# Attention with a window, then a token-mixing MLP: 1,143 steps in another written-out order

## The chip, the cores and the metric

The kernel runs on one core of a Trainium2 chip. A core has engines that run side by side, each with its own list of instructions that it works off in order: TensorE (PE in the profile; its weight loads are PEld), VectorE (DVE), ScalarE (ACT), GpSimd (POOL) and SyncE (SP), which only issues DMAs. ScalarE and GpSimd issue DMAs too. An engine waits for another by semaphores. The metric is the device time of one execution in microseconds (us), over several executions.

## What is computed

```python
# attention: B=4, H=8, S=768, D=64; window 128, 4 sink positions
scores = q @ k.T / sqrt(D)
keep = (key < 4) | ((0 <= query - key) & (query - key < 128))
a = softmax(where(keep, scores, -1e9))
x = a @ v                                   # heads side by side: (4, 768, 512)
...
a1 = alpha1 * x + beta1
tok = einsum('ts,bsd->btd', w_tok, a1)      # w_tok 768 x 768
u = x + lam * tok
a2 = alpha2 * u + beta2
ch = relu(a2 @ w_ch1) @ w_ch2               # 512 -> 2048 -> 512
out = u + lam * ch
```

Inputs and output are float32; the matmuls work on float16.

## The kernel before

The body of the kernel is a plan of 1,143 small steps, called tasks and numbered in the order in which they are described. A task is one load, one cast, a group of matmuls into one PSUM buffer, one exponential, one copy and the like. `Plan.add` describes it: what function it runs, on which engines it may run, which tasks it needs, which buffers it uses. `Plan.emit` (lines 57 to 82) walks through the tuple `ORDER` (line 216) and issues the tasks one by one. The string `ENGINES` (line 287) has one digit for each task: 0 ScalarE, 1 VectorE, 2 TensorE, 3 GpSimd, 4 SyncE. So an engine's list is `ORDER` with the other engines' tasks left out; where two neighbours in `ORDER` are on two engines, their exchange changes no list. Waits follow from the data.

The string `HOMES` (line 302) gives each buffer a slot. A buffer in a slot waits until the last user of the one before it in that slot is done. PSUM has four slots of kind `d` (`d0` to `d3`: transposes, attention output, MLP results) and two of kind `S` (scores). `n16` is a kind of SBUF buffer (four slots) in which casts of q, k and w_tok are put. `IDLES` (line 312) lays dummy matmuls on TensorE ahead of five tasks: 67 and 25 in the first 9 us, two ahead of task 109, in slot `d3`, and four and one near 28 us.

How the work runs, batch by batch:

- Queries and keys are loaded (`load_qk`, 384 KB each), cast to float16 (`trans`, line 157 on VectorE and GpSimd, 155 on ScalarE) and transposed: by TensorE (lines 508 and 511) and a copy from PSUM for batches 0 and 1, by a DMA for batches 2 and 3.
- Scores (`scores`, line 621; for the start of batch 0 in pairs, lines 682 and 685) go into an `S` slot, ScalarE takes the exponential (line 643), and the mask is put on by GpSimd (583) or VectorE (658). `pv` (lines 715, 722) multiplies by the values; VectorE divides (748). `fill_vs` (line 572) makes, by a selection matrix, the values of the sink positions.
- The token mixing (`tok`, line 853) takes 6 matmuls for each of 6 row blocks; VectorE adds (860), the result is cast to `u` (155) and transposed to `uT`, by TensorE in batch 0, by a DMA (line 912) after that, and scaled (877, 879).
- The MLP's first half (`mlp1`, line 933) makes 16 pieces of `h` for each half of the rows, four matmuls each, in a `d` slot that a relu on ScalarE (939) or VectorE (941) reads and frees. The second half is `ch` (line 1118) in batch 0; in batches 1 to 3 it is done as seven products of sums of blocks (`prod`, line 1050), in the manner of Strassen.
- The second weight comes in eight loads and is multiplied by lam in 16 pieces, `cast_w2` (line 835), each on VectorE or GpSimd. `w2_sums` (line 965) makes the sums of its blocks (`w2s`) for the products.

The four batches overlap: scores and attention of batch b+1 are laid between the MLP matmuls of batch b.

Tasks named later:

| task | what it is | engine before |
|---|---|---|
| 2 | biases from the masks (line 352) | VectorE |
| 54 | copy of a transposed k, head pair 1, batch 0 | ScalarE |
| 63 | cast of v, row blocks 0 and 1, batch 0 | VectorE |
| 43 | transpose of alpha2 and beta2 | TensorE |
| 53, 55, 59 | transposes of q and k, batch 0 | TensorE |
| 92, 95, 103, 109, 111 | scores, batch 0 | TensorE |
| 153, 157 | adding lb1 to x, batch 0 (two of `beta`) | VectorE |
| 183, 184, 202 | multiplications of w2 by lam, pieces 2, 3 and 15 | VectorE, VectorE, GpSimd |
| 262, 266, 284 | relus of batch 0 | VectorE |
| 240, 270 | relus of batch 0 | ScalarE |
| 269, 299 | `h` of batch 0, four matmuls each | TensorE |
| 352, 353 | two of the `w2s` subtractions, of groups 2 and 3 | VectorE, GpSimd |
| 372, 381 | casts of q and k, batch 1 | GpSimd |
| 395 | selection matmul of `fill_vs`, batch 1 | TensorE |
| 472 | token mixing of batch 1, row block 3, six matmuls | TensorE |
| 660 | scores of batch 2, block 1 | TensorE |
| 621 | load of a k of batch 2 | ScalarE's queue |
| 899 | cast of a k of batch 3 | ScalarE |

The lines that do the issuing:

```python
for i in order:
    t = self.tasks[i]
    e = (ACT, DVE, PE, POOL, SP)[int(engines[i])]
    ...
    for b in t.uses:
        if b.t is None:
            ...
            b.t = pool.tile(b.shape or shape, b.dtype or dtype,
                            tag=f"{b.kind}_{b.home}", bufs=1, name=b.name)
    t.fn(e)
```

Of the kernel before, what the change touches and what calls it, by code (L numbers as in the profile page):

```python
# [77 lines left out]
def kernel(  # L78
# [119 lines left out]
    for r in range(NR):  # L198
# [15 lines left out]
    PAIRS = 3  # L214

    ORDER = (
        6, 7, 0, 26, 1, 10, 5, 9, 11, 45, 18, 8, 2, 19, 48, 3, 22, 46, 15, 4, 49, 12, 50,
        17, 14, 47, 13, 16, 90, 103, 39, 41, 91, 43, 104, 53, 72, 95, 54, 28, 63, 96, 51,
        42, 73, 52, 74, 109, 100, 21, 40, 107, 44, 110, 20, 68, 108, 65, 61, 55, 92, 56, 24,
        97, 93, 101, 98, 69, 111, 94, 102, 59, 30, 62, 99, 113, 23, 57, 114, 112, 25, 116,  # L220
        105, 58, 60, 115, 27, 128, 106, 64, 131, 129, 135, 130, 125, 66, 132, 31, 138, 29,
        78, 122, 179, 117, 178, 136, 139, 126, 118, 119, 197, 140, 123, 127, 137, 120, 32,
        146, 141, 133, 84, 33, 70, 134, 79, 147, 34, 85, 144, 71, 80, 124, 86, 150, 142, 67,
        75, 35, 154, 143, 121, 151, 76, 155, 158, 148, 145, 77, 87, 152, 166, 159, 156, 81,
        167, 162, 88, 160, 163, 82, 89, 168, 149, 213, 164, 83, 153, 209, 217, 157, 214,
        218, 210, 229, 219, 211, 215, 212, 226, 165, 216, 230, 220, 161, 223, 36, 222, 232,
        221, 224, 185, 225, 177, 227, 176, 257, 169, 204, 237, 175, 233, 279, 238, 199, 234,
        258, 273, 280, 231, 259, 228, 274, 171, 277, 182, 260, 186, 241, 278, 246, 172, 200,
        295, 248, 247, 174, 291, 296, 181, 187, 243, 293, 170, 292, 242, 289, 294, 384, 267,
        188, 290, 37, 281, 268, 198, 271, 349, 282, 173, 285, 272, 358, 301, 351, 286, 180,  # L230
        378, 303, 352, 297, 302, 189, 203, 304, 249, 366, 379, 192, 190, 250, 298, 287, 369,
        380, 385, 283, 288, 375, 386, 367, 353, 265, 284, 368, 206, 370, 191, 266, 363, 376,
        381, 371, 253, 377, 299, 254, 372, 364, 300, 382, 201, 365, 373, 615, 275, 374, 383,
        205, 261, 276, 183, 357, 387, 408, 262, 263, 409, 184, 202, 395, 264, 269, 614, 411,
        239, 410, 412, 397, 240, 270, 388, 621, 396, 235, 400, 617, 196, 244, 398, 401, 355,
        255, 616, 245, 236, 390, 256, 193, 360, 389, 251, 399, 207, 311, 252, 391, 359, 335,
        393, 195, 392, 424, 208, 636, 426, 622, 194, 312, 648, 425, 336, 427, 634, 394, 428,
        413, 419, 414, 404, 420, 337, 405, 429, 402, 415, 313, 361, 422, 416, 626, 421, 441,
        305, 403, 442, 638, 640, 423, 406, 314, 619, 430, 315, 437, 443, 431, 316, 435, 641,
        338, 436, 362, 438, 306, 649, 341, 317, 432, 618, 433, 407, 637, 444, 307, 345, 439,  # L240
        644, 339, 318, 445, 620, 635, 434, 628, 450, 308, 451, 639, 440, 452, 446, 453, 417,
        642, 319, 645, 447, 340, 323, 418, 643, 320, 309, 448, 658, 623, 321, 324, 449, 322,
        329, 625, 659, 454, 646, 325, 347, 647, 330, 455, 343, 326, 344, 464, 456, 465, 348,
        466, 460, 650, 457, 467, 327, 458, 331, 629, 461, 459, 462, 653, 632, 651, 463, 656,
        332, 654, 356, 652, 660, 627, 333, 310, 342, 472, 38, 655, 624, 480, 473, 468, 469,
        470, 474, 885, 665, 471, 476, 475, 481, 482, 488, 477, 350, 483, 492, 489, 478, 490,
        657, 630, 493, 479, 514, 491, 516, 328, 515, 882, 518, 663, 880, 517, 879, 498, 666,
        661, 664, 502, 519, 499, 508, 346, 512, 662, 509, 678, 513, 484, 671, 679, 486, 676,
        503, 504, 485, 487, 354, 877, 506, 677, 672, 548, 507, 680, 526, 505, 549, 334, 674,
        546, 527, 631, 522, 681, 907, 547, 528, 523, 903, 534, 633, 529, 675, 682, 878, 890,  # L250
        535, 542, 683, 689, 543, 550, 685, 690, 510, 551, 686, 494, 511, 673, 667, 544, 495,
        891, 668, 496, 545, 901, 669, 888, 883, 693, 497, 897, 687, 684, 530, 688, 694, 700,
        531, 524, 670, 696, 701, 500, 525, 698, 697, 501, 691, 552, 699, 558, 553, 695, 704,
        562, 705, 904, 692, 559, 707, 909, 563, 706, 709, 887, 708, 564, 898, 710, 702, 566,
        565, 910, 715, 567, 703, 713, 716, 532, 714, 889, 520, 533, 717, 538, 537, 521, 921,
        539, 556, 540, 536, 557, 560, 541, 718, 899, 922, 572, 711, 881, 884, 574, 573, 896,
        712, 902, 576, 561, 719, 577, 575, 555, 727, 720, 569, 721, 580, 908, 728, 578, 581,
        729, 722, 723, 905, 579, 554, 730, 739, 568, 724, 592, 740, 725, 582, 570, 911, 726,
        588, 593, 583, 912, 584, 595, 571, 743, 731, 906, 589, 732, 585, 590, 733, 605, 900,
        587, 744, 596, 745, 606, 734, 594, 607, 611, 597, 895, 602, 612, 586, 613, 599, 603,  # L260
        591, 757, 600, 759, 758, 601, 741, 765, 742, 771, 766, 760, 916, 772, 746, 751, 917,
        773, 752, 886, 913, 761, 919, 774, 604, 767, 918, 598, 762, 763, 768, 777, 764, 779,
        920, 914, 780, 923, 915, 755, 778, 926, 608, 756, 924, 930, 735, 609, 927, 925, 931,
        753, 736, 781, 893, 737, 928, 892, 782, 934, 738, 929, 775, 935, 754, 932, 941, 610,
        769, 776, 819, 770, 894, 942, 939, 820, 821, 940, 937, 936, 823, 749, 822, 748, 945,
        824, 938, 747, 827, 933, 948, 950, 750, 943, 952, 951, 825, 953, 787, 828, 944, 807,
        788, 797, 826, 949, 808, 946, 829, 954, 798, 801, 830, 791, 802, 947, 956, 792, 783,
        957, 961, 789, 784, 962, 958, 963, 955, 790, 785, 959, 964, 811, 965, 805, 812, 786,
        795, 806, 960, 967, 796, 799, 793, 968, 970, 966, 813, 794, 969, 971, 972, 814, 815,
        973, 809, 800, 816, 974, 803, 810, 978, 804, 976, 979, 837, 975, 977, 835, 838, 980,  # L270
        841, 836, 818, 839, 843, 842, 840, 981, 845, 832, 982, 846, 817, 986, 983, 844, 831,
        990, 987, 851, 991, 988, 984, 833, 847, 992, 834, 855, 993, 848, 1002, 852, 849,
        985, 998, 1003, 989, 856, 1004, 850, 859, 1005, 1006, 860, 853, 997, 868, 995, 1007,
        996, 999, 865, 1008, 858, 857, 1000, 1009, 862, 869, 866, 874, 1001, 994, 854, 1016,
        863, 875, 1040, 1017, 871, 1041, 1038, 872, 1020, 1039, 1028, 1021, 1011, 1032,
# [2 lines left out]
        1061, 1048, 1014, 1049, 1059, 1066, 1015, 1044, 1067, 1072, 1045, 1056, 1073, 1026,  # L278
        1057, 1078, 1068, 1079, 1064, 1069, 1046, 1027, 1063, 1052, 1047, 1050, 1053, 1082,
        1051, 1062, 1084, 1083, 1065, 1030, 1080, 1085, 1101, 1031, 1081, 1091, 1102, 1107,  # L280
        1092, 1097, 1093, 1105, 864, 867, 1108, 1098, 1103, 1106, 1111, 1104, 1113, 1112,
        1089, 1114, 1115, 1086, 1116, 1090, 861, 1094, 1087, 1109, 1099, 1121, 1100, 1117,
        1095, 1110, 1125, 1118, 1122, 1134, 1124, 1123, 1126, 1128, 1135, 1127, 1088, 1119,
        1136, 1120, 1140, 873, 876, 1129, 1131, 1096, 1141, 1142, 1137, 1130, 1132, 1133,
        1138, 1139,
    )
    ENGINES = (
        "3313134433443333444444444444444433334443111211211212020212021201331121211210210200201210"
        "2020201202011202020202020213213213213213213202002020202020213121312131213121312131444444"
        "4444413114433334413314413334444042210221021021020121321021321202020020211212020202020212"  # L290
        "1212020212120202120212020212121202020202022221022221422221022221422221022221013111111331"
        "1311333333302002002132132002132002102020101212010321213120301212131201012121312010121213"
        "1203212131212131213421342104011121042104213400012120202021202021212120202020212120202121"
# [6 lines left out]
        "202020112020212021202020112020210202142141111212121212121211121112131210210214214214210"  # L300
    )
    HOMES = (
        "145602340010102001213310200221013302203140101100511203013144215120821000003330a501103130"
        "5140011112031102051467032311003221123033120133001001232002203212113003321023113113103113"
        "20311022642130030020210002112300123001450093004101001b3002014531200000131101000502017200"
        "3206010112033310021331123331330302113210001232150012232123130221212022310345033723010320"
        "103100135301020081002011411421050103321a003101204000011011051003031104020013001303110312"
        "0021102210121102223200511310123320031102032021035337572302312010320101420152002210101311"
# [1018 lines left out]
```

## Time and profile before

| | |
|---|---|
| runs before, us | 256.24, 257.22, 257.45 |
| median, us | 257.22 |
| profiled execution, us | 256.29 |
| its span (first to last instruction), us | 254.2 |
| granted TensorE clock | 0.998 |
| DMA traffic | 38.79 MB, mean 153 GB/s |

The profile cuts the span in 40 slices of 6.4 us; each digit is the busy share of a slice in tenths:

```
PE   8899999999999998999999999999999999999992
DVE  6878987778788975688889986677789885029892
ACT  2499944788986015687742445556660234643000
POOL 8527915996866516433872040066562130000010
```

Windows of 10 us of TensorE's busy time: 10.00 from 50 to 60 us, 9.64 from 60 to 70, 9.27 from 90 to 100, 10.00 from 100 to 110.

How it is read: a row of a timeline has the start, the duration, the engine, the line, the operation, what it writes and reads, and a count where several of one form follow each other. In square brackets stand the idle time before it and what ended that. Matmul records overlap, as the engine is pipelined: the step from one start to the next is what a matmul costs the list, not its record. The time of a run is some 2 us more than the span.

### The profile page before, as it was taken

The page shows a single profiled execution, that of the slowest core. Times are in us where ns is not written, and L with a number is a line of the kernel's source. Part 1 is how long each engine was busy: PE and PEld are TensorE (multiplying, and loading weights), DVE is VectorE, ACT ScalarE, POOL GpSimd, SP SyncE. Part 2 cuts the span into 40 slices and gives each one's busy share as a digit, 9 for nine tenths or more (in the row PEclk, how much of TensorE's full clock was granted, in tenths as well). Part 3 has the DMA queues.
Part 4 walks back from the last instruction along what each step waited for, and adds up shares of the span by engine and source line. Part 5 has one row for each costly group of instructions (what it writes and reads, how often), then busy time and mean ns, then how long its engine had stood idle before and what let it go on. Part 6 is the DMA issues. An engine that isn't in the chain of part 4 may idle for free.

```text
span 254.2 us, 5511 instructions
## 1 busy us (share of the span) xinstructions
PE 245.8 (97%) x2167; PEld 160.2 (63%) x2167; DVE 194.0 (76%) x400; ACT 132.5 (52%) x219; POOL 108.4 (43%) x126
## 2 busy tenths in 40 slices
PE   8899999999999998999999999999999999999992
PEld 7654655675555443566687686577577676667882
DVE  6878987778788975688889986677789885029892
ACT  2499944788986015687742445556660234643000
POOL 8527915996866516433872040066562130000010
PEclk9999999999999999999999999999999999999999
DMA  6999999999999997696476764320000141100317
GB/s 196 207 253 322 253 206 326 372 341 250 223 179 235 221 182 170 141 256 153 107 163 138 104 144 138 124 64 0 3 0 3 25 79 23 41 0 3 132 55 270
DMA packets 86129, 38.79 MB, mean 153 GB/s; under 512 B 73540, under 2 KB 80460, under 8 KB 86104
## 3 DMA queue, kind: packets, MB, share of 16 engines
q1 hardware_dynamic: 67120, 28.85, 47.7%
q10 hardware_dynamic: 15240, 6.32, 10.2%
q0 software_dynamic: 3744, 3.28, 8.1%
q8 instruction: 17, 0.28, 0.5%
q14 instruction: 8, 0.07, 0.1%
HBM read 29.91 MB, written 6.29 MB: 142 GB/s over the span
## 4 chain that ended last, share of the span: by engine, by line
PE 87%; ACT 3%; DVE 3%; DMA 3%; POOL 1%; issue 1%; POOLq 0%; ACTq 0%; DVEq 0%
PE h L933 31%; PE P L1050 22%; PE tok L853 12%; PE ch L1118 8%; PE pv L722 4%; PE S L621 4%; DMA n<-in_q_dram 3%; PE S L616 1%; PE tp L511 1%; ACT E L643 1%; ACT wt L818 1%; PE tp L508 1%; PE pv L715 1%; PE wT L813 1%; DVE w2f L835 1%
## 5 line engine op out<-in xcount | busy, mean ns | idle before, releaser
L933 PE MATMUL h<-uT,w1f 128*128 128x384 f16 x512 | 89.8, 326 | 0.4 <-DVE x L860 0.3
L933 PEld LDWEIGHTS <-w1f 128*128 128x128 f16 x512 | 48.2, 98 | 31.8 <-issue 2.2
L939 ACT ACTIVATE hT<-h 128x384 f16<-128x384 f32 x77 | 36.9, 493 | 36.2 <-PE h L933 36.0
L941 DVE TENSOR_SCALAR hT<-h 128x384 f16<-128x384 f32 x51 | 27.5, 553 | 22.6 <-PE h L933 22.2
L1050 PEld LDWEIGHTS <-hT 128*128 128x128 f16 x408 | 39.5, 98 | 7.2 <-DVE hT L993 0.6
L643 ACT ACTIVATE E<-S 128x1024 f16<-128x1024 f32 (+1 forms) x39 | 37.9, 1002 | 4.9 <-PE S L621 4.0
L766 POOL TENSOR_TENSOR tm<-x,la_b 128x512 f32<-128x512 f32 x18 | 24.6, 1369 | 22.2 <-DVE x L748 11.0
L853 PE MATMUL tok<-xh,wtokT 128*128 128x512 f16 x144 | 33.0, 379 | 0.0
L1050 PE MATMUL P<-w2f,hT 128*128 128x256 f16 x216 | 26.7, 273 | 0.0
L155 ACT CAST u<-x 128x512 f16<-128x512 f32 x17 | 10.3, 616 | 28.8 <-DVE x L860 27.3
L1063 DVE TENSOR_TENSOR x<-x,P 128x256 f32<-128x256 f32 x45 | 18.1, 417 | 7.5 <-PE P L1050 6.8
L1086 POOL TENSOR_TENSOR x<-x,pt 128x256 f32<-128x256 f32 x4 | 4.0, 997 | 46.0 <-DVE pt L1081 46.0
L1050 PE MATMUL P<-w2s,hT 128*128 128x256 f16 x192 | 23.2, 273 | 0.0
L853 PEld LDWEIGHTS <-wtokT 128*128 128x128 f16 x144 | 13.8, 98 | 14.8 <-issue 0.2
L1118 PE MATMUL ch<-w2f,hT 128*128 128x512 f16 x96 | 22.7, 379 | 0.0
L748 DVE TENSOR_TENSOR x<-pv,rec 128x256 f32<-128x256 f32 x48 | 20.4, 424 | 1.7
L155 ACT CAST n<-nat 128x768 f16<-128x768 f32 x20 | 16.2, 830 | 8.1 <-DVE xh L769 6.7
L860 DVE TENSOR_TENSOR x<-x,tok 128x512 f32<-128x512 f32 x24 | 16.0, 682 | 5.0 <-PE tok L853 4.8
L722 PEld LDWEIGHTS <-E 128*128 128x128 f16 x328 | 15.1, 98 | 5.5 <-issue 1.4
L722 PE MATMUL pv<-vfs,E 128*128 128x65 f16 x328 | 17.9, 194 | 0.0
L583 POOL TENSOR_SCALAR_AFFINE_SELECT E<-E 128x512 f16<-128x512 f16 x12 | 8.4, 723 | 17.5 <-ACT E L643 17.5
L1118 PEld LDWEIGHTS <-hT 128*128 128x128 f16 x96 | 8.8, 98 | 9.3 <-issue 0.2
(133 smaller groups left out, 346.7 us busy)
## 6 DMA issues: line engine op xcount, KB each, us to landing
wst_w<-in_moe_w_ch_dram SPq DMA_DIRECT2D x8, 512.0 KB, 8.1
nat<-in_q_dram SPq DMA_DIRECT2D x10, 384.0 KB, 4.2
nat<-in_k_dram SPq DMA_DIRECT2D x10, 384.0 KB, 8.1
vnat<-in_v_dram SPq DMA_DIRECT2D x14, 256.0 KB, 5.9
out_dram<-x SPq DMA_DIRECT2D x11, 256.0 KB, 2.9
out_dram<-x ACTq DMA_DIRECT2D x10, 256.0 KB, 3.6
wtn<-in_moe_w_tok_dram SPq DMA_DIRECT2D x6, 384.0 KB, 4.6
w1f<-in_moe_w_ch_dram POOLq DMA_DIRECT2D x4, 512.0 KB, 12.8
```

The costliest lines, as they stand in the source:

```text
L155: nc.scalar.copy(o, i)
L643: nc.scalar.activation(eT.t, pS.t[:, :, 0 : n * w].rearrange("p e (i w) -> p e i w", i=n), AF.Exp, scale=scale)
L722: nc.tensor.matmul(po.t[:, hl, :], eT.t[:, e_, off + i, c : c + P], vf[j][:, h, :], start=(r < 2 and n == 0), stop=(n == len(parts) - 1 an ...
L748: nc.vector.tensor_mul(bx.t[:, 4 * G : 4 * G + 4, :], po.t[:, :, 0:D], rec.t.to_broadcast([P, 4, D]))
L766: engine[e].tensor_mul(bt.t, bx.t.rearrange("p h d -> p (h d)"), la1_b)
L853: nc.tensor.matmul(pt.t, wtokT[:, si, ti * P : (ti + 1) * P], hs[si].t, start=(si == 0), stop=(si == NR - 1))
L933: nc.tensor.matmul(ph.t, w1f[:, c, fi * P : (fi + 1) * P], bu.t[:, c, chk * NTOK : (chk + 1) * NTOK], start=(c == 0), stop=(c == NC - 1))
L939: nc.scalar.activation(bh.t[:, fi, :], ph.t, AF.Relu)
L941: nc.vector.tensor_scalar_max(bh.t[:, fi, :], ph.t, 0.0)
L1050: nc.tensor.matmul(pc.t, hh[:, nt * P : (nt + 1) * P], w(fi), start=(first and n_ == 0), stop=(n_ == HF - 1), skip_group_check=True)
L1063: nc.vector.tensor_add(row(bx)[:, cols], row(bx)[:, cols], pc.t)
L1118: nc.tensor.matmul(pc.t, bh.t[:, fi, nt * P : (nt + 1) * P], w2f[:, fi, :], start=(fi == 0), stop=(fi == NF - 1))
```

## The change

`ORDER`, three digits of `ENGINES` and five of `HOMES` are other ones; no task is added or removed, and no function is changed. Most tasks in `ORDER` move by a few places. Read as lists of the engines:

- Engines: 54 goes from ScalarE to VectorE, 63 from VectorE to GpSimd, 202 from GpSimd to VectorE, where it stands between 262 and 184.
- TensorE: 43 goes ahead of 103, 95 ahead of 53, 92 ahead of 55, 59 ahead of 111, and some neighbours more before 31 us; 269 goes ahead of 395; 472 ahead of 660; about fifteen pairs after that, among them 522 and 546.
- VectorE: 2 goes ahead of a cast (45); 352 leaves its place after 351 and comes between 284 and 266; 354 (another such subtraction), a cast and four small steps of batch 0 and the order of 149, 153 and 157 change.
- GpSimd: 63 is new, 202 gone; two steps of batch 0 go ahead of w1 loads; the value casts 359 and 360 and a w2 multiplication (195) change places.
- ScalarE: 54 is gone; the load 621 stands ahead of the relus 240 and 270; the cast 899 three steps earlier.
- SyncE: the same list.
- Slots: 269's buffer goes from `d1` to `d0`, 395's from `d0` to `d1`; the buffer of cast 381 from `n16` slot 2 to slot 1; two small ones of kind `rec` are exchanged.

The rows of the diff that these places lie in:

```diff
-        6, 7, 0, 26, 1, 10, 5, 9, 11, 45, 18, 8, 2, 19, 48, 3, 22, 46, 15, 4, 49, 12, 50,
-        17, 14, 47, 13, 16, 90, 103, 39, 41, 91, 43, 104, 53, 72, 95, 54, 28, 63, 96, 51,
-        42, 73, 52, 74, 109, 100, 21, 40, 107, 44, 110, 20, 68, 108, 65, 61, 55, 92, 56, 24,
-        97, 93, 101, 98, 69, 111, 94, 102, 59, 30, 62, 99, 113, 23, 57, 114, 112, 25, 116,
...
-        378, 303, 352, 297, 302, 189, 203, 304, 249, 366, 379, 192, 190, 250, 298, 287, 369,
-        380, 385, 283, 288, 375, 386, 367, 353, 265, 284, 368, 206, 370, 191, 266, 363, 376,
-        381, 371, 253, 377, 299, 254, 372, 364, 300, 382, 201, 365, 373, 615, 275, 374, 383,
-        205, 261, 276, 183, 357, 387, 408, 262, 263, 409, 184, 202, 395, 264, 269, 614, 411,
-        239, 410, 412, 397, 240, 270, 388, 621, 396, 235, 400, 617, 196, 244, 398, 401, 355,
...
-        332, 654, 356, 652, 660, 627, 333, 310, 342, 472, 38, 655, 624, 480, 473, 468, 469,
...
-        539, 556, 540, 536, 557, 560, 541, 718, 899, 922, 572, 711, 881, 884, 574, 573, 896,
...
-        "3313134433443333444444444444444433334443111211211212020212021201331121211210210200201210"
-        "4444413114433334413314413334444042210221021021020121321021321202020020211212020202020212"
-        "145602340010102001213310200221013302203140101100511203013144215120821000003330a501103130"
-        "5140011112031102051467032311003221123033120133001001232002203212113003321023113113103113"
-        "20311022642130030020210002112300123001450093004101001b3002014531200000131101000502017200"
...
+        6, 7, 0, 26, 1, 10, 5, 2, 9, 11, 45, 18, 8, 19, 48, 3, 22, 15, 46, 4, 49, 12, 50,
+        14, 17, 47, 13, 16, 90, 43, 103, 39, 41, 91, 28, 72, 104, 95, 53, 54, 63, 51, 42,
+        73, 52, 21, 44, 74, 20, 96, 109, 100, 40, 107, 110, 65, 24, 68, 108, 92, 69, 55, 61,
+        56, 93, 97, 101, 98, 59, 30, 94, 102, 111, 23, 99, 62, 113, 57, 114, 25, 112, 116,
...
+        385, 206, 288, 283, 191, 375, 386, 367, 353, 265, 284, 368, 352, 370, 363, 376, 266,
+        253, 381, 377, 371, 299, 254, 372, 615, 364, 205, 300, 382, 201, 365, 373, 275, 374,
+        383, 357, 261, 276, 183, 387, 408, 262, 614, 263, 409, 202, 269, 184, 411, 410, 395,
+        264, 239, 621, 617, 412, 397, 240, 270, 388, 400, 396, 235, 616, 196, 244, 398, 401,
...
+        332, 654, 356, 472, 627, 652, 333, 342, 310, 38, 655, 660, 624, 480, 473, 468, 469,
...
+        565, 715, 910, 567, 713, 703, 716, 532, 714, 889, 520, 533, 717, 899, 538, 537, 556,
+        521, 881, 539, 884, 921, 557, 540, 536, 560, 541, 902, 718, 922, 572, 711, 574, 573,
...
+        "3313134433443333444444444444444433334443111211211212021212021203331121211210210200201210"
+        "4444413114433334413314413314444042210221021021020121321021321202020020211212020202020212"
+        "145602340010102001213310200221013302203140101100511203013044215120821000003331a501103130"
+        "5140011112031102051467032311003221123033120133001001232002203212113003320023113113103113"
+        "20311022642130030020210001112300123101450093004101001b3002014531200000131101000502017200"
```

## The prediction, made before the changed kernel was run

> **What bounds the kernel now.** I read the engines' busy times first, then what TensorE waited for, then the chain of waits, then the timelines round the two largest holes. The busy times:
>
> ```profile
> PE 245.8 (97%) x2167; PEld 160.2 (63%) x2167; DVE 194.0 (76%) x400; ACT 132.5 (52%) x219; POOL 108.4 (43%) x126
> PE 87%; ACT 3%; DVE 3%; DMA 3%; POOL 1%; issue 1%; POOLq 0%; ACTq 0%; DVEq 0%
> ```
>
> TensorE is busy for 245.8 of 254.2 us at a granted clock of 0.998, and 87% of the chain that ended last is TensorE. No matmul is added or removed, so a new order can win only where TensorE stands still, 8.4 us in all, and lose only by new holes. TensorE's waits (us in total, times, longest):
>
> ```profile
> PE idle L148 <- DVE warm L174: 1.1, 1, 1.1
> PE S L621 <- ACT E L643: 0.7, 1, 0.7
> PE S L685 <- DVE qkT L157: 0.5, 1, 0.5
> PE vsp_None L572 <- DVE hT L941: 0.4, 1, 0.4
> PE h L933 <- DVE x L860: 0.3, 1, 0.3
> PE tp L508 <- DMA n<-in_q_dram: 0.3, 1, 0.3
> PE S L616 <- ACT E L690: 0.2, 1, 0.2
> PE wT L813 <- ACT wt L818: 0.2, 1, 0.2
> ```
>
> Eight waits; the rest of the idle time is start-up and the last stores. The second lies at 98.60 us, the fourth at 60.82; the third and the last three lie before 31 us, the fifth at 41.22. The chain leaves TensorE at both of the two that the new order touches most:
>
> ```profile
> 58.85 1.45 DVE w2f L835
> 97.53 1.03 ACT E L643
> ```
>
> **Hole A, 98.60 us: gone, -0.91.** TensorE's timeline (start, us):
>
> ```profile
> 96.83 1.04 PE L1118 MATMUL ch<-w2f,hT 128*128 128x512 f16 x4
> 98.60 0.61 PE L621 MATMUL S<-qkT 64*128 64x256 f16 x8 [0.73 <-ACT E L643]
> 99.14 2.76 PE L853 MATMUL tok<-xh,wtokT 128*128 128x512 f16 x12
> ```
>
> Task 660, scores of batch 2, needs a score slot that ScalarE's exponentials free at 98.55. [...]Four ch matmuls take 0.86 (the chain has eight in 1.73), so TensorE could go on at 97.69 and stood 0.91 (0.73 by busy records). The new order puts task 472, six token-mixing matmuls (1.29 by the chain's row at 102.03), ahead of 660. By the dependences, the last thing it needs is free at 95.19, the end of VectorE's add of 94.51. It runs from 97.69 to 98.98, over the whole wait; 660 starts 0.38 later. Who waits for 660: its exponentials, which ScalarE reaches only at 106.42, so nobody. Next late could be the pv at 101.74, which needs VectorE's 1.32 mask multiply from 98.58 (ends 99.90): it moves to 100.8 and still has 0.9 to spare. After it stand matmuls h, whose inputs come through u, its transposing DMA and uT, all counted from tok matmuls that also run 0.9 earlier.
>
> **Hole B, 60.82 us: gone, -0.53.** A selection matmul (task 395) waits at 60.82, and behind it h (269), whose slot is freed by relu 262 on VectorE. VectorE's timeline:
>
> ```profile
> 41.08 0.68 DVE L835 TENSOR_TENSOR w2f<-wst_w,lam_b 128x512 f16<-128x512 f32 x1
> ...
> 58.77 1.53 DVE L835 TENSOR_TENSOR w2f<-wst_w,lam_b 128x512 f16<-128x512 f32 x1
> 60.22 0.54 DVE L941 TENSOR_SCALAR hT<-h 128x384 f16<-128x384 f32 x1
> 60.69 1.12 DVE L835 TENSOR_TENSOR w2f<-wst_w,lam_b 128x512 f16<-128x512 f32 x1
> ```
>
> and GpSimd's:
>
> ```profile
> 58.49 1.27 POOL L835 TENSOR_TENSOR w2f<-wst_w,lam_b 128x512 f16<-128x512 f32 x1
> ```
>
> The same weight multiply takes 0.68 at 41.08 and 1.53 at 58.77, beside GpSimd's own from 58.49 to 59.76. That one is task 202, which now moves to VectorE, behind relu 262. GpSimd then has nothing to do from 58.5 until the exponentials of 60.6. So task 183 ends at about 59.5, relu 262 near 60.05, before TensorE is through with h at 60.29 (59.64 + 0.65; the chain has eight h in 1.30). 269, now ahead of 395 and with slots d0 and d1 exchanged, starts at 60.29 instead of 60.82: 0.53 (0.36 by records). What it costs: 202 is 0.68 more of VectorE, 60.05 to 60.7, just before task 184, which started at 60.69 anyway. The stretch from 60 to 62 thus stays as it was, and the chain of relus behind 184 as well.
>
> **Task 352, +0.05.** This subtraction (w2s) leaves 50.26 us, where it took 1.37 (the second of two in one row of 2.21) beside GpSimd and nobody waited, and goes between relus 284 (ends 54.66) and 266 (starts 54.86). Alone it takes 0.41 (64.00). Behind it wait 266 and a qkT copy; 266 frees the slot of h 299, which TensorE starts at 56.04. The Trainium skill, "GPSIMD Engine Reference", section "8. Key points", says that GpSimd contends with VectorE instructions that have two SBUF inputs; 352 is one, and the rule speaks against this place, though it states no size. Taken as 1.37 again, 352 ends at 56.03, 266 at 56.6, and 299 stalls 0.55. But by the rows GpSimd's subtraction from 54.04 ends at 55.20, and its next cast (381) now waits for transposes that end at 55.55, because n16 slot 2 became slot 1. So 0.54 us is contended, with some 0.1 of 0.41 done in it; 352 ends near 55.5, 266 near 56.05, and 299 is 0 to 0.1 late. I take 0.05, since the row has the neighbour's end in it; 0.55 stays as the upper end. GpSimd's casts 381 and 372 end 0.45 later, at about 57.2; transposes 373 start at 57.36. Spare 0.15: nothing.
>
> **The first 31 us, 0 (-0.1 to +0.3).** The biases go ahead of a cast on VectorE; TensorE fills its time with dummy matmuls then. Copy 54 goes from ScalarE (0.80) to VectorE (0.95) and ends near 12.1 instead of 11.5; two dummy matmuls and 109 behind it come some 0.1 later. The swaps of 43, 95, 92, 55 and 111 take away the wait of 0.24 at 15.87. Yet the transpose at 17.25 needs a load that lands at 17.20: what was won ends there. Cast 63 costs GpSimd 0.6 in an idle stretch. Further on GpSimd issues the w1 loads some 0.7 earlier, but ScalarE is busy from 19.81 to 31.34 with the same list, and the token mixing at 30.48 hangs on its casts, so that wins nothing either. With the load's cover gone, the 0.24 would be won; if VectorE's delay is passed on, 0.3 lost.
>
> **Requests on ScalarE's queue, 0 (0 to +4).** The key load 621 stands two relus earlier; the trace has it at 62.64, taking 0.41 beside ScalarE's relu. Behind it now stand relus 240 and 270, whose slots TensorE needs within 1.3 us. The last reader of its buffer is long done. Load cast 899 goes some 3 us earlier, into ScalarE's idle time at 128.4 to 131.2, and frees SP's next load, on which nobody waits.
>
> **The other swaps, +0.1 (0 to +0.4).** Betas 153 and 157, value casts 359 and 360, another w2s, and some fifteen pairs on TensorE. Each operation moved forward had its inputs in before; tightest is 522, ready at 113.32 for a start at 113.40. The price of a missed one is the lateness, 0.1 or so.
>
> **The sum** against the profiled execution: 256.29 (span 254.2 and 2.1 around it) - 0.91 - 0.53 + 0.05 + 0.1 = 255.0. That execution lies 0.93 under the median of 257.22 (runs 256.24 to 257.45), so for the median **257.22 - 1.29 = 255.9 us**. What a measurement here can tell from no change is about 0.5%, 1.29 us: the forecast stands on that very line, which halves the chance of "faster".
>
> **Rivals.**
> 1. *One hole only* (0.13). A closes, for which all rows speak; B stays, if 183 is slow for another reason than 202, or 352 stalls 0.55 and eats it: 257.22 - 0.91 + 0.1 to + 0.5 = 256.4 to 256.8, say 256.6.
> 2. *Nothing* (0.06). Both are closed and the time is given back at the next transfer, as at 17.25: key and value loads, uT transposes and w2 pieces may not shift with TensorE. 257.2. Against it: TensorE's records are gapless from 31 to 240 us but for four places, so few arrivals are that close.
> 3. *Slower* (0.16): request 621 blocks ScalarE. Should it have to wait where it now stands, say for an earlier transfer, ScalarE stands with 240 and 270 behind it. ScalarE had 1.09 idle before 240, and TensorE has 1.3 of other slots, so it decides from about 2.4 us of waiting; each us beyond adds one, so from 3.7 us the whole is slower than before. These key loads take 5.5 us from issue to landing on this queue; a wait of that length costs 3.1 - 1.3 = +1.8: 259.0. Against it: in before, ScalarE's queue has no row of such a wait at 62.64.
> 4. *Better* (0.25): the 0.24 at 15.87, the 0.3 at 41.22 or the 0.5 at 9.20 shrinks too, by a swap that I priced at nothing; with the first two 255.9 - 0.54 = 255.4, with all 254.9. For it: the new order changes most lists ahead of these places. Against it: at 17.20 the load lands, and at 9.20 and 41.22 nothing that the waiting step needs comes earlier.
>
> The forecast itself has 0.40: 255.4 to 256.4. **Range** 254.7 to 258.2: from all of rival 4 to the near part of rival 3. **Chances**: faster by over 0.5% (under 255.93): half of the forecast and rival 4, 0.20 + 0.25 = 0.45. Within 0.5%: the other half, rival 1 and most of 2: 0.20 + 0.13 + 0.04 = 0.37. Slower by over 0.5% (over 258.51): rival 3 and the rest of 2, whose time may also be given back with more: 0.18.
>
> **What the changed profile would show.** A right: no wait of scores on E near 98, six tok matmuls directly after the ch at 97 and then the scores. B right: the w2f multiply near 58.8 at 0.7, h ahead of vsp without a gap, TensorE's wait on hT gone. 352: a gap before h at 56.0 under 0.1. Front: the transpose near 17.2 still at its old time. TensorE's busy sum unchanged near 245.8 and its waits shorter by 1.1. I am wrong if a new wait of over 0.3 appears, above all <-ACT hT near 62, or if a hole moves to where the next load or uT arrives.

## The result and the profile after

The changed kernel took 254.66 us in the median of 5 runs (254.39 to 255.22) beside 256.90 for the kernel before: ratio 0.9922, 95% interval 0.9896 to 0.9947. In a second comparison, with 12 runs of it against 29 of before, it took 255.63 (254.82 to 257.37) beside 256.77: ratio 0.9966, interval 0.9945 to 0.9987. Over its 17 runs the median is 255.43. Ratio and interval come from all the runs; the medians alone would give 0.9913 and 0.9956. So it is faster, by 0.3 to 0.8%; why two groups of runs of one program differ by that much is taken up at the end, and stays open in part. The profiled execution took 255.22 with a span of 253.4, against 256.29 and 254.2: 0.8 us less by spans.

The busy times and the chain after; the matmuls are the same, and the share of TensorE in the chain rises from 87 to 89%:

```profile
PE 245.6 (97%) x2167; PEld 160.4 (63%) x2167; DVE 193.6 (76%) x401; ACT 131.4 (52%) x218; POOL 107.7 (42%) x126
PE 89%; ACT 4%; DVE 4%; issue 2%; DVEq 0%; ACTq 0%
```

What TensorE waited for, after (us in total, times, longest):

```profile
PE idle L148 <- DVE warm L174: 1.1, 1, 1.1
PE wT L813 <- DVE wt L820: 0.5, 1, 0.5
PE S L685 <- DVE qkT L157: 0.5, 1, 0.5
PE idle L148 <- DVE qkT L157: 0.4, 1, 0.4
PE h L933 <- DVE x L860: 0.3, 1, 0.3
PE wT L813 <- ACT wt L818: 0.2, 1, 0.2
```

The waits of scores on E (0.7) and of vsp on hT (0.4) are gone. Two are new, on wt at 12.06 us and on qkT at 12.93.

Where the time went is best read from the start times of the same operation in both traces, as differences of after against before:

| operation on TensorE | before, us | after, us | difference |
|---|---|---|---|
| first scores (task 90) | 9.20 | 9.29 | +0.10 |
| transpose 82 | 29.97 | 30.51 | +0.54 |
| h 299 | 56.04 | 56.58 | +0.54 |
| h 239 (behind hole B) | 61.70 | 61.70 | 0.00 |
| ch 332 (ahead of hole A) | 96.83 | 96.83 | 0.00 |
| token mixing 480 (behind hole A) | 100.45 | 99.63 | -0.81 |
| h 520 | 131.01 | 130.18 | -0.83 |
| token mixing 1002 | 201.10 | 200.27 | -0.83 |

The front gives 0.54 away (0.10 of it by the later first scores), hole B gives it back, and hole A wins 0.8. Behind transpose 82 the rest of TensorE's list keeps these differences to within 0.03, but for the steps that were exchanged.

**Hole A.** TensorE's timeline after:

```profile
96.83 1.04 PE L1118 MATMUL ch<-w2f,hT 128*128 128x512 f16 x4
97.70 1.46 PE L853 MATMUL tok<-xh,wtokT 128*128 128x512 f16 x6
99.09 0.61 PE L621 MATMUL S<-qkT 64*128 64x256 f16 x8
99.63 1.47 PE L853 MATMUL tok<-xh,wtokT 128*128 128x512 f16 x6
```

No bracket stands behind the scores: the six matmuls fill the wait. From the start of tok to the start of scores it is 1.39 where 1.29 was reckoned, so the gain is 0.1 under the 0.91.

**Hole B and 352.** VectorE's timeline after:

```profile
55.11 0.91 DVE L965 TENSOR_TENSOR w2s<-w2f,w2s 128x512 f16<-128x512 f16 x1
55.94 0.55 DVE L941 TENSOR_SCALAR hT<-h 128x384 f16<-128x384 f32 x1
...
59.31 0.83 DVE L835 TENSOR_TENSOR w2f<-wst_w,lam_b 128x512 f16<-128x512 f32 x1
60.07 0.55 DVE L941 TENSOR_SCALAR hT<-h 128x384 f16<-128x384 f32 x1
60.54 1.28 DVE L835 TENSOR_TENSOR w2f<-wst_w,lam_b 128x512 f16<-128x512 f32 x2
```

and TensorE's:

```profile
60.17 1.47 PE L933 MATMUL h<-uT,w1f 128*128 128x384 f16 x8
61.48 0.38 PE L572 MATMUL vsp_None<-vfs,sel 128*128 128x512 f16 x1
```

Task 183 takes 0.83, not 1.53 (GpSimd's value cast beside it runs from 58.99 to 59.60); 202 and 184 are the pair of 1.28; eight h matmuls run through, and vsp follows without a gap. Task 352 takes 0.91, twice its 0.41 alone, because GpSimd's subtraction runs until 55.74; the relu behind it is done at 56.49, in time for h 299 at 56.58.

**The front.** VectorE after, then GpSimd, then TensorE:

```profile
9.16 1.97 DVE L1168 TENSOR_TENSOR lb_b<-lb_b,lam_r 128x512 f32<-128x512 f32 x1
11.05 0.94 DVE L820 TENSOR_SCALAR_CACHE_REDUCE wt<-wtn 128x768 f16<-128x768 f32 x1
...
11.93 0.95 DVE L157 COPY qkT<-tp 128x768 f16<-128x768 f16 x1
```

```profile
8.74 1.28 POOL L1168 TENSOR_TENSOR la_b<-la_b,lam_r 128x512 f32<-128x512 f32 x1
9.96 0.62 POOL L157 CAST vfs<-v 128x512 f16<-128x512 f32 x1
```

```profile
12.06 0.51 PE L813 MATMUL wT<-iden,wt 128*128 128x128 f16 x6 [0.53 <-DVE wt L820]
12.93 0.27 PE L148 MATMUL idle<-warm 128*128 128x128 f16 x2 [0.36 <-DVE qkT L157]
```

The cast on GpSimd at 9.96 is task 63. Before, it was not there; VectorE, then GpSimd:

```profile
9.06 1.33 DVE L1168 TENSOR_TENSOR lb_b<-lb_b,lam_r 128x512 f32<-128x512 f32 x1
8.55 1.28 POOL L1168 TENSOR_TENSOR la_b<-la_b,lam_r 128x512 f32<-128x512 f32 x1
```

The lb multiply took 1.33 and ended at 10.39, some 0.56 after GpSimd's la multiply. Now it ends at 11.13, again 0.55 after GpSimd's last, which is now the cast. Behind it in VectorE's list stand the w_tok cast, for which TensorE waits 0.53, and copy 54, for which it waits 0.36.

### The profile page after: what moved, and what is told of

The parts are those of the page before. It is cut to its first block, busy times and chain, and to the rows that moved or that the text cites. A ratio compares the mean times of both kernels' runs of the same rounds, so it can differ in the third digit from the quotient of the medians.

```text
span 253.4 us, 5513 instructions
## 1 busy us (share of the span) xinstructions
PE 245.6 (97%) x2167; PEld 160.4 (63%) x2167; DVE 193.6 (76%) x401; ACT 131.4 (52%) x218; POOL 107.7 (42%) x126
## 4 chain that ended last, share of the span: by engine, by line
PE 89%; ACT 4%; DVE 4%; issue 2%; DVEq 0%; ACTq 0%
PE h L933 32%; PE P L1050 22%; PE tok L853 12%; PE ch L1118 8%; PE pv L722 4%; PE S L621 4%; PE idle L148 2%; PE tp L511 1%; ACT wt L818 1%; ACT E L643 1%; DVE qkT L157 1%; DVE lb_b L1168 1%; PE S L616 1%; PE tp L508 1%; PE pv L715 1%
## 5 line engine op out<-in xcount | busy, mean ns | idle before, releaser
L1050 PEld LDWEIGHTS <-hT 128*128 128x128 f16 x408 | 39.3, 98 | 6.9 <-DVE hT L993 0.6
L643 ACT ACTIVATE E<-S 128x1024 f16<-128x1024 f32 (+1 forms) x39 | 37.9, 1002 | 6.9 <-PE S L621 5.9
L157 POOL CAST vfs<-vnat 128x512 f16<-128x512 f32 x18 | 13.5, 751 | 4.2 <-PE pv L722 4.2
```

The lines of the kernel that those rows point to most:

```text
L643: nc.scalar.activation(eT.t, pS.t[:, :, 0 : n * w].rearrange("p e (i w) -> p e i w", i=n), AF.Exp, scale=scale)
L1050: nc.tensor.matmul(pc.t, hh[:, nt * P : (nt + 1) * P], w(fi), start=(first and n_ == 0), stop=(n_ == HF - 1), skip_group_check=True)
```

## The experiments

All were compared with the kernel before on the same chip. The runs of one kernel spread over as much as 3.3 us, so each is read by its trace first and by its ratio second. In the traces two stretches can be compared, and all fourteen profiled executions agree on them. From transpose 82 to h 239 it is 31.7 us where 202 runs on GpSimd and 31.2 where it runs on VectorE; from ch 332 to h 520 it is 34.2 where the scores 660 stand ahead of 472 and 33.4 where they stand behind it.

### Hole A alone

```diff
-        332, 654, 356, 652, 660, 627, 333, 310, 342, 472, 38, 655, 624, 480, 473, 468, 469,
+        332, 654, 356, 652, 472, 660, 627, 333, 310, 342, 38, 655, 624, 480, 473, 468, 469,
```

> Only the six matmuls of task 472 ahead of the scores 660, all else as before. Theory (the hole at 98.6 us is closed and nothing gives it back): 0.8 to 0.9 us faster, ratio 0.9965 to 0.9970; in the profile no wait of scores on E near 98. Rival (the gain is given back at the next transfer): ratio 0.999 to 1.001, with a new wait after 100 us.

255.72 us (255.66 to 255.98) beside 256.77, ratio 0.9963, interval 0.9948 to 0.9977. The exchange closes the wait, as TensorE's timeline of this kernel shows:

```profile
97.03 1.04 PE L1118 MATMUL ch<-w2f,hT 128*128 128x512 f16 x4
97.91 1.46 PE L853 MATMUL tok<-xh,wtokT 128*128 128x512 f16 x6
99.30 0.61 PE L621 MATMUL S<-qkT 64*128 64x256 f16 x8
```

From ch 332 to h 520 it is 33.39 us, against 34.18 before and 33.35 in the changed kernel. So one exchange of two neighbours on TensorE's list is worth 0.8 us, and nothing behind it gives it back.

### Hole B alone

```diff
-        205, 261, 276, 183, 357, 387, 408, 262, 263, 409, 184, 202, 395, 264, 269, 614, 411,
+        205, 261, 276, 183, 357, 387, 408, 262, 263, 409, 202, 184, 269, 395, 264, 614, 411,
-ENGINES, task 202: 3 (GpSimd);  HOMES, h of 269: d1, vsp of 395: d0
+ENGINES, task 202: 1 (VectorE); HOMES, h of 269: d0, vsp of 395: d1
```

> Only task 202 from GpSimd to VectorE behind relu 262, and h 269 ahead of the selection matmul 395 with their two PSUM slots exchanged. Theory (the hole at 60.8 us goes because the multiply beside GpSimd's own gets fast): 0.5 us faster, ratio 0.998; the w2f multiply near 58.8 takes 0.7. Rival (VectorE's longer list passes a delay on): ratio 1.000 or over, with a later relu or mask near 62 to 64.

256.59 us (255.97 to 256.77) beside 256.77, ratio 0.9990, interval 0.9977 to 1.0004: by the clock alone this is open. The trace is not: from transpose 82 to h 239 it is 31.20 us, against 31.73 before and 31.19 in the changed kernel; 0.53 won.

### Task 202 alone

```diff
-        205, 261, 276, 183, 357, 387, 408, 262, 263, 409, 184, 202, 395, 264, 269, 614, 411,
+        205, 261, 276, 183, 357, 387, 408, 262, 263, 409, 202, 184, 395, 264, 269, 614, 411,
-ENGINES, task 202: 3 (GpSimd)
+ENGINES, task 202: 1 (VectorE)
```

> The kernel before with task 202 moved to VectorE behind relu 262, nothing else. Theory: the multiply near 58.8 takes 0.7 and relu 262 ends before TensorE is through with the h before it, so the order of 395 and 269 and their slots are not needed: from transpose 82 to h 239 31.2 us as with all three edits. Rival (395 still waits on another release of its slot): a hole of 0.1 to 0.4 stays, 31.3 to 31.6.

This kernel was run once (256.92 us), so it is read by its trace alone: 31.19 us from transpose 82 to h 239, with the old order of 395 and 269 and the old slots. VectorE's timeline:

```profile
59.96 0.68 DVE L835 TENSOR_TENSOR w2f<-wst_w,lam_b 128x512 f16<-128x512 f32 x1
60.56 0.55 DVE L941 TENSOR_SCALAR hT<-h 128x384 f16<-128x384 f32 x1
61.03 1.28 DVE L835 TENSOR_TENSOR w2f<-wst_w,lam_b 128x512 f16<-128x512 f32 x2
```

The hole was made by one multiply on GpSimd that slowed another on VectorE. Both on VectorE, one after the other, cost less than side by side: 183 has 0.68, and 202 and 184 together 1.28, where 183 and 184 alone had taken 1.53 and 1.12. The exchange on TensorE and the two slots add nothing that the trace shows.

### The front alone

```diff
-ORDER, the first 162 entries (to 30.4 us): the old ones
-ENGINES, 54: 0 (ScalarE), 63: 1 (VectorE); HOMES, rec: 1, 0
+ORDER, the first 162 entries (to 30.4 us): the new ones
+ENGINES, 54: 1 (VectorE), 63: 3 (GpSimd);  HOMES, rec: 0, 1
```

> Only the first 31 us in the new order (with tasks 54 and 63 on their new engines and the two rec slots), the rest as before. Theory (cast 63 on GpSimd slows the lb multiply on VectorE from 1.3 to 2.0 us, the w_tok cast and copy 54 queue up behind it, and the token mixing starts 0.5 later): 0.5 us slower, ratio 1.002; waits of TensorE on wt and on qkT near 12 and 13 us. Rival (the changed kernel's profiled execution was an untypical one, and the front wins in most): 0.5 to 0.9 us faster, ratio 0.9965 to 0.998.

256.76 us (255.32 to 257.40) beside 256.77, ratio 0.9992, interval 0.9975 to 1.0010. Neither the loss of the theory nor the gain of the rival shows in the runs. The trace shows a case in which nothing is lost: in this execution the first scores start at 10.27 us, not 9.20, and VectorE comes to the lb multiply only at 10.13, when cast 63 on GpSimd has 0.30 left; the multiply takes 0.85. From the first scores to transpose 82 it is 20.35 us, less than the 20.55 of the kernels with the old front. It was 21.22 in the changed kernel's profiled execution, and 20.77 before.

### All but the front

Against the changed kernel:

```diff
-ORDER, the first 162 entries: the new ones
-ENGINES, 54: 1 (VectorE), 63: 3 (GpSimd);  HOMES, rec: 0, 1
+ORDER, the first 162 entries: the old ones
+ENGINES, 54: 0 (ScalarE), 63: 1 (VectorE); HOMES, rec: 1, 0
```

> The changed kernel with the first 31 us as before. Theory (the front costs 0.5): ratio to before 0.994 to 0.995, that is 0.5 us under the changed kernel's sum of -0.83 by spans; token mixing starts at 30.3. Rival (the front wins 0.5 to 0.9): ratio 0.9945 to 0.9955 as well by the two holes alone, but then above the changed kernel's 0.9922.

255.54 us (254.82 to 257.27) beside 256.77, ratio 0.9955, interval 0.9936 to 0.9974. By the trace both holes are closed (31.21 and 33.36 in the two stretches). It is the changed kernel's second figure within the interval: without the new front nothing that can be measured is lost or won. The theory's 0.5 does not show. The rival's 0.9945 to 0.9955 was met, but it was to lie above the changed kernel's ratio, and 0.9955 lies between the two figures of that kernel.

### The changed kernel once more

> The changed kernel as it is, beside the others of this group. Theory: two holes of 0.81 and 0.53 are closed, and the first 31 us (from the first scores on) move by -0.2 where the first scores start late, by +0.45 where they start early; ratio 0.9935 to 0.9955. Rival: the 0.9922 of the first comparison stands, so 0.5 us or more are won somewhere else, ratio 0.991 to 0.993.

Ratio 0.9966, as told. The rival falls: what the first five runs had beyond the two holes did not come again. The theory's range, up to 0.9955, was missed by 0.0011 too, though the interval reaches into it. In this execution the first scores start at 9.33, yet cast 63 does not hold up the lb multiply; it is held up itself. VectorE, then GpSimd:

```profile
9.19 1.20 DVE L1168 TENSOR_TENSOR lb_b<-lb_b,lam_r 128x512 f32<-128x512 f32 x1
9.74 1.11 POOL L157 CAST vfs<-v 128x512 f16<-128x512 f32 x1
```

The multiply ends at 10.39, as before. TensorE waits on loads at 11.27, 14.98 and 17.77 us instead of on wt, and transpose 82 starts at 30.43, 0.46 later than before. So an early start is late at transpose 82 here for another reason than cast 63.

### Cast 63 back on VectorE

Against the changed kernel:

```diff
-ENGINES, task 63: 3 (GpSimd)
+ENGINES, task 63: 1 (VectorE), behind task 54
```

> The changed kernel with cast 63 back on VectorE, right behind copy 54. Theory (the cast on GpSimd beside the lb multiply cost 0.45 where the scores start early): from the first scores to the transpose 82 it takes 20.3 to 20.6 us at any start, and the wait of TensorE on wt near 12 us is at most 0.2; the median is 0 to 0.4 us under the changed kernel's. Rival (copy 54 on VectorE is what is late): 20.8 or more, and 54 still ends near 12.9 when the scores start near 9.3.

255.32 us (254.91 to 257.15) beside 256.77, ratio 0.9959, interval 0.9939 to 0.9979. In the execution that was profiled the first scores started late, at 10.70, and it is 20.35 us from there to transpose 82. That says nothing of an early start, for which the next group was made.

### Fewer dummy matmuls at the start

Against the changed kernel:

```diff
-        (46, 0, 67), (90, 1, 25), (109, 3, 2), (166, 1, 4), (162, 0, 1),
+        (46, 0, 50), (90, 1, 25), (109, 3, 2), (166, 1, 4), (162, 0, 1),
```

> The changed kernel with 50 dummy matmuls at the start in place of 67. Theory (TensorE works these off at 12 per us until its clock rises, at 3.9 to 6.3 us, and at 22 after that, so that the first transposes start anywhere from 6.4 to 7.7 and the spread of the runs comes from there): first transposes at 5.0 to 5.5 whatever the clock does, spread of the runs halved, median 0.3 to 0.9 us under the changed kernel's. Rival (the loads set the front, or the clock rises later with less work): the scores wait for loads near 11 to 17 us and the median is the changed kernel's or above.

255.99 us (254.62 to 257.02), ratio 0.9959, interval 0.9938 to 0.9981. Beside the changed kernel's 12 runs of the same group the four lowest are a little lower (254.62 to 254.76 against 254.82), the spread is 2.4 against 2.55, not half of it, and the median is not better. The first transposes start at 6.53, not at 5.0 to 5.5. The expectation had the rates wrong: dummies come 0.107 us apart until the clock rises, 9.4 in a microsecond (the 12 of a window counts those cut by its ends), so 50 of them last until 6.4 when it rises at 6.04, as here. With the first scores at 9.28 the trace has the changed kernel's wait on wt again (0.68), lb takes 1.99, and transpose 82 starts at 30.50.

The same 50 dummies were then run with three fronts, and 58 with one:

> The changed kernel with cast 63 back on VectorE and 50 dummy matmuls at the start, which makes the first scores start near 9.3 us or earlier in most executions. Theory (at an early start it is cast 63 on GpSimd that makes the lb multiply, the w_tok cast and copy 54 late): no wait on wt near 12 us, 54 ends near 12.2, and from the first scores to transpose 82 it takes 20.3 to 20.7, against 21.2 in the changed kernel's early execution. Rival (the loads bind whatever the order): 20.8 to 21.2 with waits on the load of n near 11 and 17 us.

> The changed kernel with the first 31 us as before and 50 dummy matmuls. Theory (the old front is the better one at an early start): from the first scores to transpose 82 20.5 to 20.8, median 0.2 to 0.6 us under the changed kernel's. Rival (loads near 11 and 17 us bind): as late as with 67.

> The changed kernel with copy 54 back on ScalarE and 50 dummy matmuls; cast 63 stays on GpSimd. Theory (63 is the cause, 54 only stands behind it): the lb multiply still takes 1.9 to 2.0 and TensorE waits 0.5 on wt at an early start; the wait of 0.36 before the two dummies at 13 us is gone or smaller. Rival (54 is the cause): no wait on wt, 20.3 to 20.6 from the first scores to transpose 82.

> As the first of this group with 58 dummy matmuls. Theory (each dummy fewer saves 0.056 to 0.107 us of the start until the loads bind): the median lies between those with 50 and with 67. Rival (fewer dummies let TensorE's clock fall back later on, which the granted clock of 0.992 to 0.994 in some executions with 50 points to): best of the three, with clocks over 0.995.

| front, dummies | median (range), us | ratio [interval] | first scores | lb multiply | transpose 82 |
|---|---|---|---|---|---|
| 63 on VectorE, 50 | 255.70 (254.87 to 256.51) | 0.9938 [0.9916, 0.9961] | 9.07 | 1.62 | 30.11 |
| old front, 50 | 256.06 (254.63 to 257.51) | 0.9960 [0.9935, 0.9984] | 8.75 | 1.77 | 30.18 |
| 54 on ScalarE, 50 | 255.71 (254.41 to 257.75) | 0.9945 [0.9918, 0.9972] | 8.46 | 2.07 | 30.70 |
| 63 on VectorE, 58 | 255.04 (254.62 to 255.76) | 0.9914 [0.9894, 0.9934] | 9.06 | 1.58 | 29.94 |

The kernel before took 257.13 in this group. In the two with 63 on VectorE the lb multiply ends at 10.55 and 10.51, not at 11.13, and copy 54 at 12.30 and 12.26, not at 12.88. Transpose 82 starts at 30.11 and 29.94, against 30.51 and 30.50 where 63 held lb up; 0.2 of that is the earlier start, for from the first scores it is 21.0 and 20.9, against 21.2. So far the theory holds: where cast 63 holds up the multiply, it costs some 0.2 to 0.3. But 20.3 to 20.7 was expected, and the result is what the rival said. With 50 dummies TensorE waits 0.6 on a load of n. With 58 it waits on no load, but 0.21 on wt and, as in the changed kernel, 0.36 on copy 54. The old front with 50 dummies missed its theory too: 21.4 from the first scores, not 20.5 to 20.8, with waits of 0.3 each on a load of q and one of k. In three of these four executions, then, and in the changed kernel's second, TensorE waits on loads after an early start. VectorE's timeline with 58 dummies, and GpSimd's:

```profile
8.93 1.58 DVE L1168 TENSOR_TENSOR lb_b<-lb_b,lam_r 128x512 f32<-128x512 f32 x1
10.44 0.94 DVE L820 TENSOR_SCALAR_CACHE_REDUCE wt<-wtn 128x768 f16<-128x768 f32 x1
...
11.31 0.95 DVE L157 COPY qkT<-tp 128x768 f16<-128x768 f16 x1
12.18 0.41 DVE L157 CAST vfs<-v 128x512 f16<-128x512 f32 x1
```

```profile
8.66 1.30 POOL L1168 TENSOR_TENSOR la_b<-la_b,lam_r 128x512 f32<-128x512 f32 x1
13.82 0.61 POOL L157 CAST vfs<-v 128x512 f16<-128x512 f32 x1 [3.86 <-DMA v<-in_v_dram]
```

With 54 on ScalarE the value load landed late, so cast 63 ran only at 11.02 and slowed nothing. The 2.07 of this lb multiply comes from its start at 8.32: it ends at 10.39, again 0.56 after GpSimd's la multiply. Transpose 82 was late by a load (a wait of 0.74 at 10.91) and by TensorE's clock, as the windows of this trace show (from:to in us, length, busy time and count of TensorE, its weight loads, VectorE, ScalarE, GpSimd, granted clock, DMA share, GB/s):

```profile
10.00:11.00 1.00, 0.26 (x10) 0.10 (x8) 1.00 (x2) 0.87 (x2) 0.00 (x0) 1.00 1.32 217
12.00:13.00 1.00, 1.00 (x8) 0.48 (x5) 0.63 (x3) 0.91 (x2) 0.00 (x0) 0.50 1.30 206
13.00:14.00 1.00, 1.00 (x6) 0.26 (x6) 0.89 (x3) 0.03 (x1) 0.03 (x1) 0.50 1.25 185
```

The granted clock is 0.50 there, and two matmuls of L616 take 1.06 us where they take 0.59 otherwise. TensorE had been busy for only 0.26 of the microsecond from 10 to 11. That run doesn't tell 54 and 63 apart, since the cast slowed nothing in it. Those with 63 on VectorE tell a part: without the cast beside it the multiply is early again, and the wait of 0.36 on copy 54 stays.

So with fewer dummies the clock can fall back; one profiled execution shows it, and whether the dummies are the reason is not shown. A mean clock over the span does not tell: with the old front and 50 dummies it was 0.992, and there it is 1.00 in all windows from 4 to 18 us and 0.50 from 252 to 254, behind the last matmul (248.6). The two slowest runs with 54 on ScalarE and 50 dummies (257.64 and 257.75) had 0.988 and 0.990; they were not profiled. The expectation for 58 dummies, a median between those with 50 and with 67 (255.70 and 255.32), was missed: 255.04 is below both, as its rival had it. Whether 58 is the best count stays open. As a version, 63 on VectorE with 58 dummies is the fastest that was run, 0.9914 against the changed kernel's 0.9966 and 0.9922. Its interval lies apart from that of the 12 runs and overlaps that of the 5; the two were not run in one group, so that it is the better one is likely and not shown.

## Why the prediction came out as it did

The forecast was 255.9 against 257.22, ratio 0.995, with a range of 254.7 to 258.2. The two comparisons give 0.9922 and 0.9966, the forecast between them. The first median, 254.66, lies 0.04 under the range's lower end of 254.7, the second well inside; taken as ratios to 257.22 the range is 0.990 to 1.004, and both lie in it. That the forecast falls between the two is in part luck: they are 1 us apart, and of its terms the front was wrong.

- **Hole A, -0.91**: right in mechanism, -0.81 in place of -0.91. The step from tok to scores takes 1.39, not 1.29. The trace of before had this 0.1: scores that stand behind four ch matmuls and wait for nothing start 0.96 after them, not 0.86.

```profile
95.00 1.03 PE L1118 MATMUL ch<-w2f,hT 128*128 128x512 f16 x4
95.96 0.61 PE L621 MATMUL S<-qkT 64*128 64x256 f16 x8
```

  So 0.81 of the 0.91 was a wait, and the rest a price of scores behind such matmuls in either order.
- **Hole B, -0.53**: right, -0.54 in the changed kernel, -0.53 alone. The reason was right too (183 slowed by 202), but the exchange of 269 and 395 and the slots, which the prediction let share in it, are not needed.
- **Task 352, +0.05**: right; 0.00 (h 273 to h 299 takes 14.82 us before and after). Its time was 0.91, between the 0.41 and the 1.37 that were weighed. The rule that GpSimd contends with it holds, and it costs nothing since the contention ends with GpSimd's subtraction.
- **First 31 us, 0 (-0.1 to +0.3)**: the step that failed. "Cast 63 costs GpSimd 0.6 in an idle stretch" looked at GpSimd's list alone. GpSimd was idle there, but VectorE was in its lb multiply, which ended 0.74 later; copy 54 ended at 12.88, not 12.1, for the same reason. From the first scores to transpose 82 it cost 0.45, beyond the stated +0.3. Cast 63 is put at 0.2 to 0.3 of it by the two fronts with 63 on VectorE, one execution of each. The rest may be copy 54, which was priced at 0.1 and for which TensorE waits 0.28 to 0.36 in every trace of the new front with 54 on VectorE in which no load came late; that is not shown. In the second execution of the changed kernel the delay came with waits on loads. At a late start the new front wins some 0.2 (20.35 against 20.55): the load is there in time, and the wait for which the prediction had named 0.24, at 15.87 before, is 0.14 with the old front at a late start and gone with the new one.
- **Requests on ScalarE's queue, 0**: right. The trace of after has the request 621 between two exponentials, at 60.37, taking 0.41, with no wait; rival 3 is out.
- **The other swaps, +0.1**: 0.00; from h 520 to token mixing 1002 it is 70.09 us in both traces.
- **The sum**: -1.29 was forecast. The traces give -0.81 - 0.54 + 0.54 = -0.81 at an early start and, as a sum of stretches from several kernels, about -0.81 - 0.53 - 0.2 = -1.5 at a late one; no late execution of the changed kernel itself was profiled. The medians differ by -2.24 in the first comparison and -1.14 in the second, so the runs do not decide between these sums.

The view that would have shown the failed step was in hand: VectorE's row at 9.06, 1.33 for the lb multiply, where a multiply of the same size takes 0.68 at 41.08, beside GpSimd's la multiply from 8.55 to 9.83. It was slowed already, and the cast went to where it had just become free.

## What to carry to other kernels

When one engine bounds at 97%, look for its few waits and for work of its own list that is ready and long enough to stand in each; that was worth 0.8 us for one exchange. Before work goes to an idle engine, look at what its neighbour does in that stretch: two multiplies side by side on GpSimd and VectorE cost more than the same two in a row on VectorE, and a stretch in which one of the two is idle isn't free. Where runs spread as widely as a change is worth, compare start times of the same operation across traces, stretch by stretch, and let the ratio confirm it.

## What was not expected of the hardware

**TensorE's clock rises at another time in each execution, and the front follows.** The kernel starts with 67 dummy matmuls from 1.06 us on. In each trace they start 0.107 us apart at first and 0.056 apart from some moment on. That moment was 3.91 us before, 4.12 and 4.21 in the two executions of the changed kernel, 4.77, 6.15, 6.44, 6.47, 6.87 and 7.09 in others. So the first transposes behind the dummies start at 6.45 to 7.96 us and the first scores at 9.20 to 10.70. Windows of before, and of the kernel with 63 on VectorE and 67 dummies (columns as in the windows above):

```profile
5.00:6.00 1.00, 1.00 (x22) 1.00 (x20) 0.86 (x4) 0.40 (x1) 0.92 (x4) 1.00 0.97 275
```

```profile
5.00:6.00 1.00, 1.00 (x12) 1.00 (x11) 0.63 (x2) 0.40 (x1) 0.92 (x4) 1.00 1.07 343
```

22 matmuls against 12 in the same microsecond, with a granted clock of 1.00 in both: the column doesn't show it; the count does. The Trainium skill, "TensorE: Matmul & The Clock Gate", section "What's actually happening", tells of two clock states, a free-running window of 3.4 us that the start of a kernel does not reset, and a warm-up of one busy window; the distances of 106.7 and 55.6 ns that its section "Wait — 56ns, not 53.3ns?" gives for such a matmul are those of the traces. It gives the transition a variation of half a microsecond either way, where these traces have 3.2 us between the earliest and the latest, about the length of its window, and 2.85 us for the shortest warm-up. Of the 1.4 us between the first scores of an early and of a late execution (9.20 and 10.60) 1.2 reach transpose 82 (29.97 against 31.16 with the old front), and with it the end.

**The last stores take another time too.** In the profiled executions with 50 dummies, with 63 on VectorE and with the old front, VectorE's last add ends at 249.00 and 249.07, earlier than the 249.28 of the changed kernel. Yet their spans are 254.4 and 254.9 against 253.4: after that add come only the stores of the output, for 5.4 and 5.9 us against 4.1. So part of the spread is not the front's; how much of the medians with fewer dummies it makes is not shown.

Whether these two causes make the 1 us between the groups of five and of twelve runs is not shown. Both profiled executions of the changed kernel had an early rise, and took 255.22 and 255.39; the other four of the first five runs were faster than that, down to 254.39, and no trace shows why.

**VectorE's multiply of two SBUF operands ends when GpSimd lets it.** Before, after, and with 63 on VectorE and 50 or 58 dummies, the lb multiply started at 8.93 to 9.16 and took 1.33, 1.97, 1.62 and 1.58; where GpSimd was done it took 0.68. It ended each time 0.55 or 0.56 after the end of GpSimd's last operation beside it, that is with most of its own 0.68 still to do. Task 183 before fits too: it ended 0.54 after 202. In one execution, the changed kernel's second, it was the other way round for the cast: the multiply ended 0.56 after GpSimd's la multiply, and the cast took 1.11 in place of 0.62. What decides which of the two goes first is not shown.
